# A fused attention and feed-forward kernel: first h of chunk 0 taken ahead, fp32 dummies, a new order at the end of chunk 0, and kv and num rows of 66 columns for 65

## Chip, cores, metric

One core of one Trainium2 chip. The metric is device time in microseconds (us) of one execution. The profile's "span" is about 1.8 us shorter than that time: it leaves out what lies before the first and after the last recorded instruction.

## The reference

```python
# attention with a cosine weight, linear in the sequence: B, H, S, D = 8, 8, 576, 64
theta = pi/2 * arange(S) / S
phi(x) = concat([relu(x)*cos(theta), relu(x)*sin(theta)])     # 2*64 features
kv  = einsum('bhsf,bhsd->bhfd', phi(k), v)
num = einsum('bhsf,bhfd->bhsd', phi(q), kv)
den = einsum('bhsf,bhf->bhs',  phi(q), sum_s phi(k)) + 1e-6
x   = (num/den) as (4608, 512)
# feed-forward: d_model 512, d_ff 2048
h = x @ w_in;  g = h * sigmoid(beta*h);  out = g @ w_out
```

## The kernel before

The 4608 tokens go through the feed-forward part in nine chunks of 512 (chunk 0 to 8), and PE has the attention of the next batch cut in between the chunk's matmuls. A chunk has 32 slots: 16 groups of h (four matmuls of 512 columns each) and 16 of o. The parts that the change and the argument touch:

```python
E = D + 1                       # a row of kv or num: 64 values and the sum for den

def kv_mm(b, jp, bank):         # 72 matmuls a batch, 64x64, 2*E = 130 columns
    ...
def num_mm(n, jp, bank, slot):  # four 64x64 quadrants of PE, cosine half then sine half
    for cs in range(2):
        for jj in range(2):
            for g in range(2):
                nc.tensor.matmul(ps[cols, bank + jj, slot*E : (slot+1)*E],
                                 lhsT=(qt, qs)[cs][rows, jp, n, cols],
                                 rhs=kv[rows, g, jp, cs, :], start=(cs == 0), stop=(cs == 1))

HB = (0, 1, 4, 5)               # PSUM banks of h
def h_bank(c, jt):
    return ((3, 2, 6, 7), (2, 3, 0, 1))[c][jt] if c < 2 and jt < 4 else HB[jt % 4]

def o_part(c, tt, part):        # four of the sixteen matmuls of one o tile;
    ...                         # after the last part ScalarE copies it out (o_sb), then a store

warm_pe(58, 48)                 # PE dummies while the first loads come
...
for gj in GJ: cast_win(0, gj, "pool", jps=slice(0, 1))        # first w_in to bf16, GpSimd
x_turn_pe(0, 0, 8, 2, jps=(0,))                               # x of chunk 0, behind num 1
...
early = { ...
    26: lambda: (takes.append(q_turn_pe(1, 1, 6, hold=True)),
                 [takes[0](*t) for t in turns], cast_wout(3, "addd"),   # last quarter of w_out
                 [takes[1](*t) for t in turns]),
    28: lambda: (num_seven(0, 4), x_mul(x_rden(4, 0, 0, 7, (0,)), 0, 7)),
    29: lambda: (num_seven(1, 6), x_mul(x_rden(6, 0, 0, 7, (1,)), 0, 7)),
    30: lambda: x_turn_pe(1, 0, 7, 4, ("act",), (0,)),        # x of chunk 1
    31: ... }
for slot in range(32):          # chunk 0
    if slot < 4:    h_mm(0, slot, (2, 3)); h_act(0, slot)
    elif slot < 16: h_group(0, slot)
    else:           o_part(0, slot % 4, (slot - 16) // 4)     # w_out arrives by quarters
    ...
    if slot in early: early[slot]()
```

## Time and profile before

| what | before |
|---|---|
| device time | 296.05 us, median of 3 (295.56 to 296.68) |
| span of the profiled run | 294.3 us |
| PE busy | 284.1 us, 97% |
| a chunk in the steady part (chunks 2 to 6) | 30.34 us |
| last quarter of w_out landed, first matmul on it | 45.20 us, 45.99 us |

First the start: PE's timeline. The columns are start (us), length (us, up to the modelled end of the last one), engine, line, operation, destination <- sources, shapes, and the count of instructions run together.

```profile
16.29 0.62 PE L340 MATMUL ps<-ident,xs 128*128 128x128 bf16 x8
...
18.02 0.59 PE L366 MATMUL ps<-xt,win 128*128 128x512 bf16 x2
```

L340 turns x, L366 is h. The first h starts at 18.02. Then the busy time of the engines in the stretch around the end of chunk 0, where the prediction finds its three holes (columns: window; its length, then busy us and instructions of PE, of PE's weight loads, of VectorE, ScalarE and GpSimd; granted clock; DMA share; GB/s):

```profile
45.00:57.00 12.00, 10.74 (x194) 5.51 (x195) 8.31 (x18) 7.26 (x12) 4.33 (x8) 1.00 0.86 317
```

PE is idle for 1.26 us of these 12.

### The profile page before, as it was taken

The page shows a single profiled execution, that of the slowest core. Times are in us where ns is not written, and L with a number is a line of the kernel's source. Part 1 is how long each engine was busy: PE and PEld are TensorE (multiplying, and loading weights), DVE is VectorE, ACT ScalarE, POOL GpSimd, SP SyncE. Part 2 cuts the span into 40 slices and gives each one's busy share as a digit, 9 for nine tenths or more (in the row PEclk, how much of TensorE's full clock was granted, in tenths as well). Part 3 has the DMA queues.
Part 4 walks back from the last instruction along what each step waited for, and adds up shares of the span by engine and source line. Part 5 has one row for each costly group of instructions (what it writes and reads, how often), then busy time and mean ns, then how long its engine had stood idle before and what let it go on. Part 6 is the DMA issues. An engine that isn't in the chain of part 4 may idle for free.

```text
span 294.3 us, 7183 instructions
## 1 busy us (share of the span) xinstructions
PE 284.1 (97%) x3046; PEld 143.2 (49%) x3074; DVE 116.6 (40%) x297; ACT 140.1 (48%) x223; POOL 73.8 (25%) x88
## 2 busy tenths in 40 slices
PE   8799999999999999999999999999999999999995
PEld 7454455455444544454444544554455444444444
DVE  5989968662920294009500860077005000000000
ACT  5768826572248214831384128511761177127611
POOL 1350003252382026402460156014701210000000
PEclk9999999999999999999999999999999999999999
DMA  7999999597898089925992599239201910131033
GB/s 258 373 391 381 389 390 391 192 286 275 159 280 348 2 110 222 374 86 111 210 392 79 102 226 379 82 63 181 64 2 33 159 37 0 38 71 36 0 73 72
DMA packets 50416, 53.82 MB, mean 183 GB/s; under 512 B 30912, under 2 KB 31312, under 8 KB 50384
## 3 DMA queue, kind: packets, MB, share of 16 engines
q1 hardware_dynamic: 47424, 45.88, 51.7%
q0 software_dynamic: 2688, 7.34, 10.1%
q8 instruction: 24, 0.39, 0.5%
q10 hardware_dynamic: 272, 0.14, 0.2%
q14 instruction: 8, 0.07, 0.1%
HBM read 36.71 MB, written 9.44 MB: 157 GB/s over the span
## 4 chain that ended last, share of the span: by engine, by line
PE 84%; DVE 5%; DMA 5%; ACT 2%; issue 2%
PE ps L366 38%; PE ps L391 37%; DMA w_stage<-in_moe_w_out_dram 5%; DVE win L108 4%; PE ps L281 4%; PE ps L260 3%; PE ps L406 1%; PE ps L415 1%; ACT vb L213 1%; DVE qs L218 1%; DVE xs L303 0%; ACT g_t L373 0%; ACT rk L188 0%; PE ps L424 0%; PE ps L230 0%
## 5 line engine op out<-in xcount | busy, mean ns | idle before, releaser
L366 PE MATMUL ps<-xt,win 128*128 128x512 bf16 x576 | 128.1, 379 | 0.7 <-ACT g_t L373 0.5
L391 PE MATMUL ps<-wout,g_t 128*128 128x512 bf16 x535 | 120.4, 379 | 2.5 <-issue 1.4
L373 ACT ACTIVATE g_t<-ps,beta 128x512 bf16<-128x512 f32 x144 | 98.5, 688 | 36.5 <-PE ps L366 36.5
L366 PEld LDWEIGHTS <-win 128*128 128x128 bf16 x576 | 55.3, 98 | 67.5 <-DVE win L108 1.4
L391 PEld LDWEIGHTS <-g_t 128*128 128x128 bf16 x560 | 54.0, 98 | 64.0 <-issue 0.5
L386 POOL DMA_DIRECT2D out_dram<-o_sb x56 | 36.5, 656 | 142.2 <-ACT o_sb L397 142.2
L397 ACT COPY o_sb<-ps 128x512 f32<-128x512 f32 x35 | 20.5, 587 | 98.2 <-PE ps L391 98.2
L218 POOL TENSOR_TENSOR qs<-qt,tanr 128x1152 bf16<-128x1152 bf16 x12 | 29.2, 2456 | 10.3 <-DVE vb L215 8.9
L272 DVE CAST kv<-ps 128x520 bf16<-128x520 f32 x6 | 4.2, 699 | 67.8 <-PE ps L260 67.8
L409 DVE COPY o_sb<-ps 128x256 f32<-128x256 f32 (+1 forms) x2 | 0.7, 358 | 62.6 <-PE ps L406 62.6
L303 DVE TENSOR_TENSOR xs<-ps,rden 128x768 bf16<-128x768 f32 (+5 forms) x26 | 23.1, 890 | 0.8
L292 DVE TENSOR_TENSOR den<-ps,eps 128x12 f32<-128x12 f32 (+4 forms) x26 | 4.2, 161 | 33.5 <-PE ps L281 33.5
L215 DVE TENSOR_SCALAR vb<-raw_v,cos 128x256 bf16<-128x256 f32 x63 | 17.1, 348 | 0.0
L215 DVE TENSOR_SCALAR vb<-raw_v,sin 128x256 bf16<-128x256 f32 x54 | 14.7, 350 | 0.0
L281 PEld LDWEIGHTS <-qt 64*64 64x64 bf16 x576 | 10.6, 106 | 5.0 <-issue 4.3
L281 PE MATMUL ps<-kv,qt 64*64 64x65 bf16 x576 | 11.8, 194 | 0.4 <-ACT kv L270 0.2
L190 DVE TENSOR_SCALAR qb<-raw_q 128x1152 bf16<-128x1152 f32 x16 | 11.4, 753 | 1.3 <-DMA raw_q<-in_q_dram 1.3
L108 DVE CAST win<-w_stage 64x512 bf16<-64x512 f32 (+1 forms) x28 | 11.6, 413 | 0.6
L281 PE MATMUL ps<-kv,qs 64*64 64x65 bf16 x576 | 11.6, 193 | 0.0
L260 PE MATMUL ps<-vb,rk 64*64 64x130 bf16 x576 | 10.0, 218 | 1.6 <-ACT rk L188 1.6
L260 PEld LDWEIGHTS <-rk 64*64 64x64 bf16 x576 | 8.5, 106 | 5.6 <-issue 3.0
L281 PEld LDWEIGHTS <-qs 64*64 64x64 bf16 x576 | 10.4, 105 | 0.0
(56 smaller groups left out, 99.3 us busy)
## 6 DMA issues: line engine op xcount, KB each, us to landing
raw_v<-in_v_dram SPq DMA_DIRECT2D x7, 1152.0 KB, 10.3
raw_k<-in_k_dram SPq DMA_DIRECT2D x7, 1152.0 KB, 12.7
raw_q<-in_q_dram SPq DMA_DIRECT2D x7, 1152.0 KB, 7.5
out_dram<-o_sb POOLq DMA_DIRECT2D x56, 128.0 KB, 4.0
w_stage<-in_moe_w_out_dram SPq DMA_DIRECT2D x4, 1024.0 KB, 9.1
w_stage<-in_moe_w_in_dram SPq DMA_DIRECT2D x3, 1024.0 KB, 13.0
out_dram<-o_sb SPq DMA_DIRECT2D x14, 128.0 KB, 2.3
raw_q<-in_q_dram SPq DMA_DIRECT2D x2, 576.0 KB, 4.4
```

The source lines that it names most:

```text
L108: nc.vector.tensor_copy(o, a)
L190: nc.vector.tensor_scalar(dst, src, scalar1=0.0, scalar2=None, op0=ALU.max)
L215: nc.vector.tensor_scalar(o, a, scalar1=t[:, n : n + 1], scalar2=None, op0=ALU.mult)
L218: eng.tensor_tensor(dst.rearrange("q n (g p) -> q n g p", g=2), src.rearrange("q n (g p) -> q n g p", g=2), tanr[:, n0:n1].unsqueeze(2).to ...
L260: nc.tensor.matmul(t[jj * HP : (jj + 1) * HP, g], lhsT=rk[hs, n, 2 * jp + jj, :], rhs=vb[hs, n, 2 * jp + jj].rearrange("q s e -> q (s e)") ...
L281: nc.tensor.matmul(ps[cols, bank + jj, slot * E : (slot + 1) * E], lhsT=(qt, qs)[cs][rows, jp, n, cols], rhs=kv[rows, g, jp, cs, :], start ...
L303: nc.vector.tensor_tensor(o.rearrange("q j n s d -> q j (n s) d"), nv[:, :, a:z, :, 0:D].rearrange("q j n s d -> q j (n s) d"), rden[:, :, ...
L366: nc.tensor.matmul(ps[:, h_bank(c, jt)], lhsT=win[jt // 4][:, mi, (jt % 4) * P : (jt % 4 + 1) * P], rhs=xt[:, :, jp, g * HP : (g + 1) * HP ...
L373: nc.scalar.activation(g_t, ps[:, h_bank(c, jt)], AF.Silu, scale=beta[:, jt : jt + 1])
L386: eng.dma_start(out=out_v[bb, n][:, m0:m1], in_=o_sb[hf * HP : (hf + 1) * HP, m0:m1])
L391: nc.tensor.matmul(o_ps, lhsT=gs[c, jt][:, tt * P : (tt + 1) * P], rhs=wout[jt // 4][:, jt % 4, :], start=(jt == 0), stop=(jt == JT - 1))
L397: nc.scalar.copy(o_sb, o_ps)
```

## The change

Its intent: start h of chunk 0 earlier (fp32 dummies fill PE before that), close the holes where chunk 0 passes into chunk 1, and make the rows of kv and num an even number of columns so that all of them start on an even address.

```diff
-    E = D + 1
+    E = D + 2
+    nc.vector.memset(vb.rearrange("q n j s e -> q (n j s) e")[:, :, D + 1], 0.0)
@@ banks of h
-        return ((3, 2, 6, 7), (2, 3, 0, 1))[c][jt] if c < 2 and jt < 4 else HB[jt % 4]
+        if c < 2 and jt < 4:
+            return ((3, 2, 0, 1), (6, 7, 2, 3))[c][jt]
+        return ((6, 7, 4, 5) if c == 0 else (4, 5, 0, 1))[jt % 4]
@@ start
-    warm_pe(7)
+    warm_long(4)                          # four fp32 matmuls of 256 columns
...
+    x_turn_pe(0, 0, 4, 4, jps=(0,))       # x of chunk 0 ahead of num 1
+    x_turn_pe(0, 4, 8, 5, jps=(0,))
     for n in range(7):
         num_mm(n, 1, 0, n)
     num_mm(7, 1, 6, 0)
-    for gj in GJ:
-        cast_win(0, gj, "pool", jps=slice(0, 1))
...
-    x_turn_pe(0, 0, 8, 2, jps=(0,))
+    for gj, eng in zip(GJ, ("pool", "dve", "pool", "dve")):
+        cast_win(0, gj, eng, jps=slice(0, 1))
+    for gj, eng in zip(GJ, ("dve", "pool", "pool", "pool")):
+        cast_win(0, gj, eng, jps=slice(1, 2))
...
@@ end of chunk 0
-        [takes[0](*t) for t in turns], cast_wout(3, "addd"),
+        [takes[0](*t) for t in turns], cast_wout(3, "adda"),
-    30: lambda: x_turn_pe(1, 0, 7, 4, ("act",), (0,)),
...
+        elif slot < 28:
+            o_part(0, slot % 4, (slot - 16) // 4)
         else:
-            o_part(0, slot % 4, (slot - 16) // 4)
+            for tt in (2 * (slot % 2), 2 * (slot % 2) + 1):
+                o_mm(0, tt, range(12, 14) if slot < 30 else range(14, 16),
+                     (lambda: x_turn_pe(1, 0, 7, 4, ("act",), (0,))) if tt == 0 else None)
```

(Cut: h in two blocks of columns, the split of v's scaling, slots 4 and 9 for 3 and 7, num_rest in bank 0, three fewer dummies, and the place of a few VectorE casts.)

## The prediction

> **What bounds the kernel now.** I read the page first, then the chain of waits, then the timelines of the stretches that the change touches.
>
> ```profile
> span 294.3 us, 7183 instructions
> PE 284.1 (97%) x3046; PEld 143.2 (49%) x3074; DVE 116.6 (40%) x297; ACT 140.1 (48%) x223; POOL 73.8 (25%) x88
> PE   8799999999999999999999999999999999999995
> DMA  7999999597898089925992599239201910131033
> ```
>
> PE is at work from end to end; no other engine is near it. From chunk 2 on the chain is PE alone, one chunk every 30.34 us (124 to 154 us, say), with no wait but the switches between the 128-wide and the 64-wide matmuls. So a gain can only be work taken from PE, or a PE hole closed in the first 57 us. The second thing to see is the DMA row: sevens and nines in its first seven slices, the first 50 us. There the kernel also loads 15 MB. The chain of waits, in order of time, says what that does:
>
> ```profile
> 31.44 13.76 DMA w_stage<-in_moe_w_out_dram
> 45.22 0.73 ACT wout L115
> 45.99 1.02 PE ps L391 x4
> ...
> 50.16 0.46 issue
> 50.62 0.92 ACT xt L345
> 51.59 1.02 PE ps L366 x4
> ...
> 55.27 1.27 ACT g_t L373 x2
> 56.59 7.93 PE ps L366 x36
> ```
>
> Three PE holes stand here. By the starts of the matmuls: one of 0.385 us before 45.99 (start-to-start 601 ns where 216 is the pace), where PE wants the last quarter of w_out, landed at 45.20 and scaled on ScalarE until 45.94; one of 0.39 us before 51.59 (606 ns), PE waiting for ScalarE's copy of x of chunk 1, which had stood behind a copy of o_sb; and one of 0.655 us before 56.59 (871 ns), PE waiting for a silu to release bank 0. Ahead of 45.99 the load is no bubble: its issue at 31.44 queues behind others. The landings before it come at 33.06, 36.08, 38.78, 41.80 and 45.20, each about 3 us for about 1 MB, and the bandwidth stays at 380 to 400 GB/s. The first 45 us are therefore a race of two streams, and the DMA stream wins it by 0.385 us.
>
> For the rows of 65 I looked at the 64-wide matmuls of one steady chunk; four quadrants run side by side, so a line of four is one step:
>
> ```profile
> 101.42 0.20 PE L281 MATMUL ps<-kv,qt 64*64 64x65 bf16 x4
> 101.45 0.20 PE L281 MATMUL ps<-kv,qs 64*64 64x65 bf16 x4
> 101.49 0.20 PE L281 MATMUL ps<-kv,qt 64*64 64x65 bf16 x4
> 101.52 0.20 PE L281 MATMUL ps<-kv,qs 64*64 64x65 bf16 x4
> 101.55 0.20 PE L281 MATMUL ps<-kv,qt 64*64 64x65 bf16 x4
> ...
> 101.68 0.20 PE L281 MATMUL ps<-kv,qt 64*64 64x65 bf16 x4
> ```
>
> Eight steps from 101.42 to 101.68, some 32 ns each. In nanoseconds the steps repeat with a period of four: 29, 35, 33, 32. Of these the 29 is the cosine half (a kv row at an even column) into an even slot of PSUM; the three others have an odd start in kv, in PSUM, or in both.
>
> **What the Trainium skill says.** (1) TensorE: Matmul & The Clock Gate, Back-to-back issue gap: a warm matmul of N columns takes N/2.4 + 2.5 ns. The trace agrees: 216 ns at 512, 56 at 128, and the kv steps of 130 columns 56.7. For 65 it gives 29.6, which only the aligned step shows. (2) Advanced Engine Details and Errata, PSUM Cachelines and SBUF Cachelines: PSUM lines are 8 bytes, two fp32 values, and SBUF lines 16 bytes. It doesn't say what an odd start costs; the 29 against 32 to 35 above fits it, with two causes not told apart. (3) Advanced Engine Details and Errata, VectorE Performance Modes: the two-port mode wants SBUF on both sides and even outer dimensions. So I do not expect rows of 66 to speed up the scaling of v: its 256 columns at 348 ns are 215 ns fixed and 133 at two a cycle, the same fixed part as 482 ns for 512 columns of wout gives, so it is fast already. (4) DMA: Bandwidth & Descriptors, Issuing engines are not separate DMA queues: all loads share the same 16 engines and interleave, from which I take it that an earlier issue into a full queue brings nothing. The row of nines agrees.
>
> **The change part by part.**
>
> *Rows of 66.* A num step becomes (66+6)/2.4 = 30.0 ns, always aligned, against a mean of 32.3 in the first 20 steps of a chunk and 33.4 in the last 16 (mean 32.8): 2.8 x 36 = 0.10 us less per batch. A kv step goes from 56.7 to 57.5 (two more columns): 0.8 x 18 = 0.015 more. Net 0.085 us per batch; batch 0 lies ahead of the DMA wait, so seven count: -0.6 us. The added memset (72 columns; a 64-column one took 0.11 us) falls into VectorE's 0.38 us idle before 4.36. The copies of kv, 528 columns for 520, are some 8 ns longer.
>
> *Start of chunk 0.* Before: x of the first half goes through PE at 16.29, ScalarE copies it until 18.0, h starts at 18.02, and the sixteen matmuls of the first four h groups end at 21.9. After: x is transposed in two parts ahead of num 1 (VectorE's product, 1.08 us from 14.35, is split as well), ScalarE copies from about 15.6 to 16.8 in two copies of 0.59, and the four casts of w_in that it needs (0.61 each on GpSimd, from 14.87) are shared with VectorE (0.42). So h may start at about 16.9. VectorE pays: three casts ahead of den of num 1 move that from 16.36 to about 16.8, so x of the second half is there at 20.0, against 19.5 before; the split of h into blocks lets half of the rest begin at 19.3. I get the sixteen done at about 21.0: 0.9 us earlier. GpSimd's two added slices of v (1.47 us becomes 1.96) end at 10.9, where k, landed 10.30, holds ScalarE's relu until about 11.1 anyway. The fp32 dummies fill a stretch in which PE waits. Then the sum: of these 0.9 us, nothing arrives. PE then stands before w_out's last quarter 1.3 us instead of 0.385, since the load still lands near 45.2 (15 MB at the same rate, same order of issue) and the first cast still ends at 45.94. I set this part at 0.
>
> *End of chunk 0, start of chunk 1.* From 45.99 on PE has the same matmuls in another order. The first two of each o group go first, and the transposes of x stand after the first group's last two, at about 49.5, with ScalarE's copy ahead of all o_sb copies. That copy is done at about 51.0 while PE is busy until 51.2: the hole of 0.39 closes. Chunk 1's first groups use banks 6, 7, 2, 3 and the fifth bank 4, idle since that copy: the hole of 0.655 closes. Given back: ScalarE now has two casts of w_out (0.63 apart) ahead of the second q copies; VectorE loses one of 0.4, but waits for ScalarE at the last piece, so qs ends at 48.0 rather than 47.83 and the product for x about 0.2 later, of which some 0.1 reaches PE. Net -0.9 us.
>
> Sum: -0.6 - 0.9 = -1.5 us, 296.05 to 294.5.
>
> **The rivals.** (a) The early start does come through, because w_out lands sooner. For it: that landing took 3.4 us where 1 MB usually takes 2.7, with an instruction fetch of 16 KB at 42.9 on one DMA engine, so the landing can move by 0.7. Against: PE's program has as many instructions, so the fetch comes again. It would give 293.6. (b) The holes after 46 us only shift: VectorE's product for x becomes the wait at 49.5, or the fifth h waits for something else. ScalarE is at 4 us in 5 there, but not full. It would give 295.3. (c) The slow num steps come from the weight loads of 64 columns, not from odd starts, so that 66 is no better and costs 0.12 us of kv and 0.1 of num in all. Against: the 29 ns step has the same weight loads. It would give 295.3. (d) PE gets behind: a VectorE cast waiting for the second part of w_in (landed 16.18) holds x of num 1. It has over 1 us of slack at the DMA wait, so it would cost nothing.
>
> **Range and chances.** The middle is 294.5. Rivals a, b and c span 293.6 to 295.3, and single runs of the kernel before span 1.1 us, so 293.5 to 295.6 should hold it 8 times in 10. Faster by over 2% would be under 290.1, over four times the gain that I find anywhere: 0.02. Slower by over 2% needs a new wait of 6 us: 0.02. Within 2%: 0.96.
>
> **What would show it.** Num steps at 30 ns without the period of four; steady chunks at 30.25 us instead of 30.34; the first h at about 16.9 and the fifth h group at about 21; a PE hole before the last quarter of w_out that has grown to over 1 us, with that matmul again at about 46.0; no holes of 0.4 us at 51 and 0.65 at 56. I am wrong if that matmul starts well before 45.5, if num steps stay at 32 to 33, or if chunk 1's fifth h group still waits for ScalarE.

## The result, and the profile after

The changed kernel took 295.96 us, median of four runs (295.83 to 296.0); the kernel before 296.0 (295.56 to 296.68). A ratio here is the mean time of one kernel's fast runs over the mean of the other's in the same rounds, so not quite the ratio of the medians: 0.9996, 95% interval 0.9976 to 1.0015. That is the same within 2%, as predicted, but the time lies outside the predicted range of 293.5 to 295.6. Of the 1.5 us, next to nothing arrived.

Lines of the page after, for those that the prediction shows of before:

```profile
span 294.1 us, 7240 instructions
PE 285.8 (97%) x3080; PEld 144.4 (49%) x3080; DVE 116.8 (40%) x297; ACT 139.7 (47%) x223; POOL 74.3 (25%) x85
```

The chain of waits after, in order of time (start, length, what):

```profile
30.95 14.29 DMA w_stage<-in_moe_w_out_dram
45.26 0.73 ACT wout L115
46.04 1.02 PE ps L392 x4
...
51.42 0.86 PE ps L367 x4
...
54.37 9.17 PE ps L367 x42
...
101.70 1.62 PE ps L392 x7
103.93 9.87 PE ps L392 x45
...
132.83 11.33 PE ps L392 x52
```

Up to 54.37 this is the prediction: w_out again lands at 45.24 and sets PE's start at 46.04; then no copy of x at 50.6 and no silu at 55.3 stands in the chain any more. (The 54.37 here is a modelled time; by its start it is 54.30. The same matmul started at 54.63 before, and after six matmuls PE waited until 56.59 for the silu.) The stretch's busy time says the same:

```profile
45.00:57.00 12.00, 11.59 (x200) 5.85 (x199) 8.14 (x17) 8.00 (x14) 4.58 (x8) 1.00 0.89 299
```

PE now idles 0.41 us in it instead of 1.26; what is left is the wait for w_out. (The two windows don't hold quite the same work; by the same matmul, the first of kv in chunk 2, the kernel after is 1.07 us ahead: 93.83 against 94.90.)

The unexpected thing is one line further down. The last 52 matmuls of o of a chunk run in one piece in chunks 3 to 6 ("x52"), but in chunk 2 they are broken at the eighth, 101.70 to 103.93. PE's timeline there:

```profile
101.64 1.69 PE L392 MATMUL ps<-wout,g_t 128*128 128x512 bf16 x7
103.93 2.32 PE L392 MATMUL ps<-wout,g_t 128*128 128x512 bf16 x10 [0.61 <-issue]
```

The seventh starts at 102.94, the eighth at 103.93: 986 ns where 216 is the pace, so 0.77 us are lost inside one accumulation, with weights, operands and bank long there. "issue" means that the profile finds nothing that PE waited for. But the DMA view of 101.2 to 102.6 us holds one packet, and it isn't data:

```profile
q8 instruction: 1, 0.02, 5.6%
```

5.6% of 16 engines over 1.4 us is 1.25 us of one engine: an instruction fetch of 16 KB, from 101.28 to 102.52 in the trace. The kernel before has one too, at 102.33 to 103.55, and no hole behind it. After this hole the lead is 0.30 us (kv of chunk 3 at 124.95 against 125.25).

One half of the num matmuls, by groups, first before, then after (columns: busy us, mean ns of one from its own start to its end, so not the pace):

```profile
L281 PE MATMUL ps<-kv,qt 64*64 64x65 bf16 x576 | 11.8, 194 | 0.4 <-ACT kv L270 0.2
L282 PE MATMUL ps<-kv,qt 64*64 64x66 bf16 x576 | 11.7, 195 | 0.2 <-ACT kv L271 0.2
```

The busy time is as good as unchanged. Counted by starts, the 144 num matmuls of a steady chunk take 1.237 us before and 1.237 us after, and the steps still repeat 29, 35, 33, 32 ns. The 72 of kv take 0.999 us before and 1.012 us after.

The start after, on PE:

```profile
16.82 1.03 PE L367 MATMUL ps<-xt,win 128*128 128x512 bf16 x4
18.65 0.40 PE L341 MATMUL ps<-ident,xs 128*128 128x128 bf16 x4 [0.81 <-DVE xs L304]
```

The first h is at 16.82, as predicted (16.9), but then PE loses 0.97 us waiting for VectorE's x (the profile counts 0.81 idle, as ends are modelled). By the starts of the matmuls, the first four h groups are done at 21.94, not at the predicted 21.0, and even 0.2 us later than before (21.74). The first o of chunk 0 is at 32.77 instead of 32.99, and PE stands before the last quarter of w_out at 45.46 instead of 45.605: inside, 0.15 us arrived where 0.9 was predicted, and the hole before w_out is 0.58 us instead of the predicted 1.3.

The whole account, in us, between the two profiled runs:

| term | predicted | measured |
|---|---|---|
| rows of 66: num | -0.7 | 0.00 |
| rows of 66: kv | +0.1 | +0.09 (seven times 0.013) |
| start of chunk 0 | 0 | 0 |
| end of chunk 0 | -0.9 | -1.05 |
| last quarter of w_out, first matmul on it | 0 | +0.05 |
| hole in chunk 2 | not in the sum | +0.77 |
| a like stall in chunk 1, only before | not in the sum | -0.11 |
| sum | -1.5 | -0.25 |
| span | | -0.22 (294.27 to 294.05) |

The stall in chunk 1 is in num: 1.351 us before and 1.238 after; before, PE stops there for 0.11 us, 1.4 us after a fetch landed at 70.65. 0.03 us of the difference of the spans are not accounted for.

### The profile page after: what moved, and what is told of

Its sections match the earlier page's. It is cut to its first block, busy times and chain, and to the rows that moved or that the text cites. A ratio compares the mean times of both kernels' runs of the same rounds, so it can differ in the third digit from the quotient of the medians.

```text
span 294.1 us, 7240 instructions
## 1 busy us (share of the span) xinstructions
PE 285.8 (97%) x3080; PEld 144.4 (49%) x3080; DVE 116.8 (40%) x297; ACT 139.7 (47%) x223; POOL 74.3 (25%) x85
## 4 chain that ended last, share of the span: by engine, by line
PE 83%; DMA 8%; DVE 5%; issue 1%; SPq 1%; ACT 1%
PE ps L392 38%; PE ps L367 38%; DMA w_stage<-in_moe_w_out_dram 5%; DVE win L108 4%; PE ps L282 3%; DMA raw_v<-in_v_dram 3%; PE ps L261 2%; PE ps L412 1%; DVE xs L304 1%; SPq L78 1%; ACT vb L214 0%; DVE rden L297 0%; PE ps L341 0%; ACT wout L115 0%; DVE den L293 0%
## 5 line engine op out<-in xcount | busy, mean ns | idle before, releaser
L367 PE MATMUL ps<-xt,win 128*128 128x512 bf16 (+1 forms) x584 | 127.8, 376 | 0.1
L392 PE MATMUL ps<-wout,g_t 128*128 128x512 bf16 x560 | 124.7, 379 | 1.0 <-issue 0.6
L367 PEld LDWEIGHTS <-win 128*128 128x128 bf16 x584 | 56.4, 98 | 65.1 <-issue 0.4
L387 POOL DMA_DIRECT2D out_dram<-o_sb x56 | 38.0, 683 | 145.7 <-ACT o_sb L400 145.7
L273 DVE CAST kv<-ps 128x528 bf16<-128x528 f32 x6 | 4.2, 707 | 67.9 <-PE ps L261 67.9
L219 POOL TENSOR_TENSOR qs<-qt,tanr 128x1152 bf16<-128x1152 bf16 x12 | 28.5, 2398 | 6.4 <-DVE vb L216 6.3
L108 DVE CAST win<-w_stage 64x512 bf16<-64x512 f32 x27 | 12.0, 443 | 0.6
L191 DVE TENSOR_SCALAR qb<-raw_q 128x1152 bf16<-128x1152 f32 x16 | 11.4, 752 | 1.3 <-DMA raw_q<-in_q_dram 1.3
L261 PE MATMUL ps<-vb,rk 64*64 64x132 bf16 x576 | 10.3, 219 | 1.7 <-DVE rk L191 0.8
L282 PE MATMUL ps<-kv,qt 64*64 64x66 bf16 x576 | 11.7, 195 | 0.2 <-ACT kv L271 0.2
L282 PE MATMUL ps<-kv,qs 64*64 64x66 bf16 x576 | 11.5, 193 | 0.0
```

The lines of the kernel that those rows point to most:

```text
L108: nc.vector.tensor_copy(o, a)
L191: nc.vector.tensor_scalar(dst, src, scalar1=0.0, scalar2=None, op0=ALU.max)
L219: eng.tensor_tensor(dst.rearrange("q n (g p) -> q n g p", g=2), src.rearrange("q n (g p) -> q n g p", g=2), tanr[:, n0:n1].unsqueeze(2).to ...
L261: nc.tensor.matmul(t[jj * HP : (jj + 1) * HP, g], lhsT=rk[hs, n, 2 * jp + jj, :], rhs=vb[hs, n, 2 * jp + jj].rearrange("q s e -> q (s e)") ...
L282: nc.tensor.matmul(ps[cols, bank + jj, slot * E : (slot + 1) * E], lhsT=(qt, qs)[cs][rows, jp, n, cols], rhs=kv[rows, g, jp, cs, :], start ...
L367: nc.tensor.matmul(ps[:, h_bank(c, jt), blocks.start * 64 : blocks.stop * 64], lhsT=win[jt // 4][:, mi, (jt % 4) * P : (jt % 4 + 1) * P], ...
```

## The experiments

Two questions: is the hole in chunk 2 the fetch, and why do rows of 66 do nothing? For the hole, theory 1: a line of 256 PE instructions comes late, so the hole stands at a fixed count of instructions and moves when PE has more or fewer of them ahead of it. The rival: the hole belongs to what the change does with data (the wider rows, the new banks), and then goes away with that and not with the count. For the rows, the prediction's step (an odd start costs, so an even one gains) stands against its own rival (c): the weight loads of 64 columns set the pace. A third question, later: is the early start really worth nothing, or only because something else is in the way?

"Faster", "same" and "slower" below are ratios to the kernel before in the same rounds; none reaches 2%, so all are "same" in the class of the prediction. Runs a were on one chip, b and d1 on a second, c on a third: compare runs of different letters by the ratio. What every run gave:

| run | median us (runs) | ratio to before, 95% interval | loss at the hole in chunk 2 |
|---|---|---|---|
| a1_after_again | 295.71 (5) | 0.9979, 0.9966 to 0.9992 | 0.45 us, eighth o matmul |
| a2_rows65 | 295.54 (5) | 0.9981, 0.9969 to 0.9993 | 0.48 us, eighth |
| a3_before_rows66 | 295.75 (5) | 0.9994, 0.9982 to 1.0005 | none |
| a4_shift64 | 298.03 (6) | 1.007, 1.0048 to 1.0092 | none |
| b1_end_only | 294.87 (6) | 0.9954, 0.994 to 0.9968 | none (0.18 in chunk 5) |
| b2_dummies51 | 297.44 (6) | 1.0047, 1.0029 to 1.0064 | none |
| b3_dummies63 | 295.26 (4) | 0.9971, 0.9953 to 0.999 | none |
| b4_sine40 (wrong result) | 296.2 (1) | | 1.08 us, eighth |
| c1_start_only63 | 295.91 (5) | 0.9996, 0.9981 to 1.0011 | 0.27 us, third |
| c2_fill | 294.99 (6) | 0.996, 0.9943 to 0.9978 | none |
| c3_casts_pool | 295.63 (1) | | 0.32 us, fourth |
| d1_start_fill | 295.19 (6) | 0.9973, 0.9958 to 0.9988 | 0.32 us, third |

### a1: the changed kernel again

No edit; five rounds, for the size of the difference and to see whether the hole comes again.

> The changed kernel once more, for a second profile and a narrow interval. In its first profile PE was 1.05 us ahead of the kernel before from 57 us on, and lost 0.77 us of it in one hole at 103 us, between two matmuls of one group. Theory 1 (a hole of the instruction supply, tied to the place in the program): the hole is there again, at 103 us, 0.6 to 0.9 us long; time 295.9. Theory 2 (a chance event): no hole there, or one elsewhere; then 295.2. Theory 3 (the profile of before was a slow sample and there is no gain at 57 us): the fifth group of h in chunk 1 starts less than 0.5 us ahead of the kernel before in the same job.

295.71 us (294.99 to 295.96): faster by 0.2%, and this interval leaves 1 out. The hole is there again, ahead of the same eighth matmul: the seventh starts at 103.14, the eighth 668 ns later, 0.45 us lost (0.6 to 0.9 was expected). So it is no accident of one execution, and its size varies: the fetch was from 101.45 to 102.41.

### a2 and a3: the rows alone

```diff
 # a2: the changed kernel
-    E = D + 2
+    E = D + 1
-    nc.vector.memset(vb.rearrange("q n j s e -> q (n j s) e")[:, :, D + 1], 0.0)
 # a3: the kernel before
-    E = D + 1
+    E = D + 2
+    nc.vector.memset(vb.rearrange("q n j s e -> q (n j s) e")[:, :, D + 1], 0.0)
```

> The changed kernel with rows of 65 again and without the memset; all else as changed. If rows of 66 cost nothing but two more columns in kv, kv takes 0.999 us for 72 matmuls rather than 1.012 and the num phase 1.237 us as with 66; time 0.1 us below the changed kernel (295.8). If odd starts cost what the prediction said, the num phase is 0.1 us longer than with 66: the two profiles already speak against it. The PE hole at 103 us: with theory 1 at the same place (the PE program is unchanged, row for row); with theory 2 it need not be.

> The kernel before with rows of 66 alone. Only kv grows, 13 ns per batch: 296.1, so same within noise. The prediction's step of -0.6 us would give 295.4; a num phase at 1.14 us rather than 1.237 would be its sign, and I no longer expect that.

Both give 1.237 us for the num phase of a steady chunk, with 65 columns as with 66; kv takes 0.999 us with 65 and 1.012 with 66. The hole is in a2 (rows of 65, ahead of the eighth matmul) and not in a3 (rows of 66), so it isn't the rows. a3 has the two holes of the old end of chunk 0 again, 0.389 and 0.653 us. Its 295.75 against 296.08 leave 1 inside the interval: rows of 66 alone are worth nothing that can be told from zero.

### a4 and b2: more and fewer instructions ahead

```diff
 # a4: the changed kernel
     warm_long(4)
+    warm_pe(32, 32)          # 64 PE instructions more
 # b2: the changed kernel
-    warm_pe(58, 48)
+    warm_pe(51, 55)          # 14 fewer, about the same time
```

> The changed kernel with 32 more dummies of 32 columns in a stretch of the start in which PE waits for k (idle from 10.0 to 10.84 us). They cost nothing there (32 x 25 ns = 0.8 us, before a wait of which PE has over 0.5 us to spare at the wait for w_out), but move all later PE instructions 64 places on. Theory 1: the hole at 103 us moves or goes; if it goes, 295.2. Theory 2: no telling. If PE is just late by the dummies: no change of the time, since the wait for w_out takes it.

> The changed kernel with 51 dummies of 55 columns in place of 58 of 48 at the very start: as many columns, 14 PE instructions fewer, so that those of chunk 2 stand where they stand in the kernel before. Theory 1 (the hole at 103 us depends on where the num phase of chunk 2 lies in the blocks of 256 instructions in which they are fetched): no hole, 0.45 to 0.77 us less than the changed kernel, 295.2. If the hole had to do with anything else that the change did (banks, order, rows of 66), it stays, and 295.9.

In both the hole in chunk 2 is gone, as theory 1 has it, but both missed on the time: 298.03 and 297.44 us, slower by 0.7% and 0.5%. A hole stands in the start instead, behind another fetch, and costs more there. The PE timeline of b2 shows it inside the 36 matmuls of one kv:

```profile
14.09 0.62 PE L261 MATMUL ps<-vb,rk 64*64 64x132 bf16 x20 [0.51 <-ACT rk L189]
17.10 0.66 PE L261 MATMUL ps<-vb,rk 64*64 64x132 bf16 x16 [2.39 <-issue]
...
20.08 1.91 PE L367 MATMUL ps<-xt,win 128*128 128x512 bf16 x4
```

The fetch there ran from 14.55 to 15.68. In a4 the hole is 2.3 us, from 16.6 on:

```profile
19.05 1.50 PE L367 MATMUL ps<-xt,win 128*128 128x512 bf16 x4 [2.10 <-DVE xs L304]
```

with the fetch from 16.48 to 17.57. (VectorE, the releaser named, can't be what held it: this is the first h, which in the changed kernel starts at 16.82 with the same casts done.) And there is a second cost: the clock falls to half and PE runs at half pace until about 23 us, 427 ns for a matmul of 512 columns (in b2 the four of 20.08). The granted clock of b2 shows it, in the page's row of 40 slices; the third is 14.8 to 22.2 us:

```profile
PEclk9969999999999999999999999999999999999999
```

### b3: ten instructions more

```diff
-    warm_pe(58, 48)
+    warm_pe(63, 44)
```

> The changed kernel with 63 dummies of 44 columns, 10 PE instructions more. Theory 1 says more here: the hole stays at the same instruction of the program's count, so it moves from ahead of the eighth o matmul after num of chunk 2 to ahead of the third, some 1.1 us earlier in chunk 2, and is again 0.4 to 0.8 us long, because the fetch starts as much earlier. Time as the changed kernel, 295.7 to 296.0. A hole still ahead of the eighth speaks against it.

295.26 us. The expected hole ahead of the third matmul was not in this profile: its fetch was at 99.22, before num began, instead of 101.28. c1, c3 and d1 have the same 63 dummies, and there it is, ahead of the third or fourth matmul, so five (in c3 four) matmuls of two instructions each earlier than the eighth: where ten more instructions ahead put it (in c3 eight more, as PE has two semaphore waits fewer ahead).

With all runs that have the hole, in us:

| run | fetch landed | PE goes on | between | PE instructions ahead |
|---|---|---|---|---|
| after | 102.52 | 103.93 | 1.41 | 2753 |
| a1 | 102.41 | 103.81 | 1.40 | 2753 |
| a2 | 101.75 | 103.12 | 1.37 | 2753 |
| b4 | 102.92 | 104.35 | 1.43 | 2753 |
| c1 | 101.43 | 102.88 | 1.45 | 2753 |
| c3 | 101.49 | 102.86 | 1.37 | 2753 |
| d1 | 100.71 | 102.04 | 1.33 | 2753 |
| b2, in the start | 15.68 | 17.10 | 1.42 | 450 |
| a4, in the start | 17.57 | 19.05 | 1.48 | 707 |
| b1, in chunk 5 | 192.25 | 193.59 | 1.34 | 4802 |

The last column counts PE's records in the trace (matmuls, weight loads, semaphore waits) that start before the matmul that goes on. It is the same in all seven runs with the hole in chunk 2, whatever their order, banks and rows are, and the four numbers differ by multiples of 256, within two (2753 - 450 is 9 x 256 - 1). That is theory 1 in the traces themselves: PE stands where one line of 256 gives way to the next. The stalls in num of chunk 1 (0.01 to 0.08 us in a2, b3 and c1) stand behind 1985 instructions, 3 x 256 fewer than 2753.

PE goes on 1.33 to 1.48 us after the fetch has landed, wherever it lies. In b3 that would be about 101.5, and its third matmul was due at about 101.67, so no hole. In the kernel before, the fetch landed at 103.55, ready at about 104.95 by the same rule; PE has 14 instructions fewer ahead, so the place is the fifteenth matmul, due at about 105.7: no hole either. The changed kernel's 14 more instructions bring the place forward by seven matmuls, 1.5 us, and that is more than there was in hand. Why the place after num is the tight one is argued, not shown: num's 144 matmuls and 144 loads pass in 1.237 us, so that 256 instructions last about 1.1 us there (an estimate from this), no longer than a fetch.

### b4: num with 40 columns in the sine half (wrong result)

If odd starts or the number of columns set the pace of num, steps of 40 columns must be much shorter. The result is wrong (relative error 0.38).

```diff
+                    e0 = 26 * cs
-                        ps[cols, bank + jj, slot * E : (slot + 1) * E],
+                        ps[cols, bank + jj, slot * E + e0 : (slot + 1) * E],
-                        rhs=kv[rows, g, jp, cs, :],
+                        rhs=kv[rows, g, jp, cs, e0:E],
```

> Wrong on purpose: the changed kernel with the sine half of num adding only 40 of its 66 columns. If a num step is set by the columns that it streams, sine steps fall from 33 ns to (40+6)/2.4 = 19 ns, the num phase from 1.237 us to about 1.0. If it is set by the weight loads, the sine steps stay at 32 to 35 ns and the phase at 1.237 us; then neither rows of 66 nor starts at even columns could have made it faster.

The num phase took 1.234 us instead of 1.237. PE's timeline:

```profile
101.28 0.22 PE L283 MATMUL ps<-kv,qt 64*64 64x66 bf16 x4
101.31 0.21 PE L283 MATMUL ps<-kv,qs 64*64 64x40 bf16 x4
101.34 0.22 PE L283 MATMUL ps<-kv,qt 64*64 64x66 bf16 x4
```

Steps of 40 and of 66 columns alternate, and each takes 31 to 34 ns; by columns the 40 would take 19. So neither the columns nor the even start sets the pace. (The period of four is gone here, 31 or 32 ns in most of the first 20 steps, while the sum stays: what makes that pattern is open.) What stays is the stream of weight loads, one of 64 columns for each matmul; that they are the bound is the one explanation left of those considered, not something that a run took away. A rival to it was not tested: the rate at which PE takes instructions, eight a step, so about 4.1 ns each.

### b1: the end of chunk 0 alone

The kernel before, with its start and rows of 65, and only the new banks of chunk 1's h, the new order of o, the transposes of x between, num_rest in bank 0 and the last cast on ScalarE.

```diff
-    26: ... cast_wout(3, "addd"), ...
+    26: ... cast_wout(3, "adda"), ...
-    30: lambda: x_turn_pe(1, 0, 7, 4, ("act",), (0,)),
+        else:                             # slots 28 to 31
+            for tt in (2 * (slot % 2), 2 * (slot % 2) + 1):
+                o_mm(0, tt, range(12, 14) if slot < 30 else range(14, 16), ...)
```

> The kernel before with only the end of chunk 0 changed (order of the last o matmuls, x transposed ahead of the o_sb copies, other banks for chunk 1, casts of w_out). Its PE program has as many instructions ahead of chunk 2 as the kernel before, so no hole at 103 us is expected (theory 1). If this part is the whole gain, the two holes of 0.39 and 0.65 us at 51 and 56 us go and the time is 1.0 us below the kernel before: 295.0. If the new start is needed for it, less than 0.5 us.

294.87 us (294.34 to 295.29), faster by 0.46% (0.3 to 0.6): the lowest ratio of all versions (the interval of c2 overlaps it), better than both kernels. No hole at 51, at 56 or in chunk 2, in PE's timeline:

```profile
50.08 1.46 PE L391 MATMUL ps<-wout,g_t 128*128 128x512 bf16 x6
51.37 1.03 PE L366 MATMUL ps<-xt,win 128*128 128x512 bf16 x4
...
101.72 3.63 PE L391 MATMUL ps<-wout,g_t 128*128 128x512 bf16 x16
```

PE has as many instructions ahead of chunk 2 as the kernel before (1214 weight loads ahead of its num in both; 1220 in the changed kernel, and these six pairs of load and matmul with two more waits are its 14), so the fetch is in time. This is the predicted -0.9 by itself: -1.17 by the medians (296.04 to 294.87).

### c1: the start and the rows, without the end

The changed kernel with the old end of chunk 0 and 63 dummies.

```diff
-            return ((3, 2, 0, 1), (6, 7, 2, 3))[c][jt]
-        return ((6, 7, 4, 5) if c == 0 else (4, 5, 0, 1))[jt % 4]
+            return ((3, 2, 0, 1), (2, 3, 0, 1))[c][jt]
+        return ((6, 7, 4, 5) if c == 0 else (0, 1, 4, 5))[jt % 4]
-    warm_pe(58, 48)
+    warm_pe(63, 44)
...  # and the hunk "end of chunk 0" of the change taken back
```

> The changed kernel with the end of chunk 0 as before (order, banks, casts), and with 63 dummies of 44 columns, whose count showed no hole in chunk 2: so the new start, the fp32 dummies and rows of 66 alone. The prediction set the start at 0 because PE waits for the last quarter of w_out anyway. If that holds: 296.0, same as the kernel before within 0.2%, with both holes of 0.39 and 0.65 us at 51 and 56 us back. If the start brings something of its own: 295.5 or less.

295.91 us against 296.25, ratio 0.9996: the start is worth nothing that can be told from zero. The chain shows the two old waits, ScalarE's copy of x and the silu:

```profile
50.17 0.92 ACT xt L346
...
51.14 1.02 PE ps L367 x4
...
54.82 1.27 ACT g_t L374 x2
```

(lost: 0.391 and 0.655 us, as before the change). In this profile w_out landed at 44.61, and PE didn't wait for it; what an earlier landing gave, the hole of 0.27 us in chunk 2 and kv's wider rows took in part.

### c3: all eight casts of the first w_in on GpSimd

Why did the early start arrive only with 0.15 us? In the changed kernel VectorE's timeline has its three casts at 15.59, beside GpSimd's:

```profile
15.59 1.93 DVE L108 CAST win<-w_stage 64x512 bf16<-64x512 f32 x3
```

They took 0.42, 0.72 and 0.72 us, where 0.42 each was predicted, so den came at 17.44 instead of 16.8. GpSimd's own went from 0.61 to between 0.69 and 0.77.

```diff
-    for gj, eng in zip(GJ, ("pool", "dve", "pool", "dve")):
+    for gj, eng in zip(GJ, ("pool", "pool", "pool", "pool")):
         cast_win(0, gj, eng, jps=slice(0, 1))
-    for gj, eng in zip(GJ, ("dve", "pool", "pool", "pool")):
+    for gj, eng in zip(GJ, ("pool", "pool", "pool", "pool")):
         cast_win(0, gj, eng, jps=slice(1, 2))
```

(with 63 dummies)

> The changed kernel, 63 dummies, with all eight casts of the first part of w_in on GpSimd. In the changed kernel VectorE's three casts beside GpSimd's took 0.42, 0.72 and 0.72 us and GpSimd's 0.69 to 0.77 where they take 0.42 and 0.61 alone. If the two hinder each other, GpSimd's casts are back at 0.61 us here, and VectorE's den of num 1 starts at about 16.4 to 16.8 us rather than at 17.4; h then starts at about 17.7 for want of GpSimd's fourth cast. If the casts are slow for another reason (the load of w_in landing at the same time), GpSimd's casts stay at 0.7 us.

VectorE's timeline in c3, the den of num 1:

```profile
16.69 0.17 DVE L293 TENSOR_TENSOR den<-ps,eps 128x14 f32<-128x14 f32 x1 [1.09 <-PE ps L282]
```

GpSimd's casts went back to 0.60 to 0.61 us and den to 16.69. But the first h at 16.85 then waits 0.67 us for GpSimd, so little is won inside; VectorE's later casts of w_in were again slow (0.85, 0.74) as long as GpSimd worked beside them, and 0.42 when it had stopped. The two engines hinder each other here; dividing the casts between them doesn't give the sum of their speeds. The time, 295.63 in one run, can't tell anything.

### c2 and d1: filling the wait for w_out

If PE stands before w_out, give it other work. The num of the first half of batch 1 goes ahead of the last quarter of o. c2 has this on top of b1 (old start), d1 on top of the new start with rows of 65 and 63 dummies.

```diff
-            return ((...), (6, 7, 2, 3))[c][jt]
+            return ((...), (4, 2, 3, 6))[c][jt]
     26: lambda: (..., [takes[0](*t) for t in turns], cast_wout(3, "adda"),
-                 [takes[1](*t) for t in turns]),
-    28: lambda: (num_seven(0, 4), x_mul(x_rden(4, 0, 0, 7, (0,)), 0, 7)),
-    29: lambda: (num_seven(1, 6), x_mul(x_rden(6, 0, 0, 7, (1,)), 0, 7)),
+    27: lambda: (num_seven(0, 4), x_mul(x_rden(4, 0, 0, 7, (0,)), 0, 7),
+                 [takes[1](*t) for t in turns]),
+    30: lambda: (num_seven(1, 6), x_mul(x_rden(6, 0, 0, 7, (1,)), 0, 7)),
```

> A version that should beat both: the kernel before with the changed end (which gave 294.87), and num of batch 1's first half (0.68 us of PE work that needs no w_out) moved ahead of the wait for w_out, VectorE's product for x with it; chunk 1's first four groups in banks 4, 2, 3, 6 so that none waits for num's second half. PE has some 0.3 to 0.6 us to fill there, so 294.3 to 294.6. If the product for x or the second q copies become the wait instead, 294.9 as without it.

> The changed kernel with rows of 65, 63 dummies in place of 58, and the num of the first half of batch 1 moved from behind the last quarter of w_out to ahead of it (about 0.9 us of PE work), so that PE has something to do while it waits there. In runs with the new start PE arrives at 45.46 and waits 0.15 to 0.7 us, depending on when the load lands; in the run with the old start and the same filling there was nothing to fill, and it gained nothing over the end alone (294.99 against 294.87). If the early start of 0.15 us plus the wait can be turned into work, this gives 294.4: no PE hole over 0.1 us at 45 to 46, and the fifth h group of chunk 1 0.3 to 0.5 us earlier against the landing than in the changed kernel. If VectorE and ScalarE, which have to copy q and cast w_out in the same 2 us, set the end of chunk 0 instead, PE waits again at 47 to 50 and it gives 294.9 to 295.3, no better than the end alone. The hole of the fetch in chunk 2: 0 to 0.3 us with 63 dummies.

c2 missed: 294.99, no better than b1's 294.87 (ratios 0.996 and 0.9954). With the old start PE reaches w_out when its cast is as good as done, so there is no wait to fill. d1 missed its 294.4 too: 295.19, inside the range of its rival theory but not for the rival's reason. The mechanism did work in its profile, as PE's timeline shows (the num in front of 46.28 begins at 45.64):

```profile
46.28 2.32 PE L391 MATMUL ps<-wout,g_t 128*128 128x512 bf16 x10
...
53.97 3.19 PE L366 MATMUL ps<-xt,win 128*128 128x512 bf16 x14
...
101.28 0.60 PE L391 MATMUL ps<-wout,g_t 128*128 128x512 bf16 x2
102.04 3.18 PE L391 MATMUL ps<-wout,g_t 128*128 128x512 bf16 x14 [0.16 <-issue]
```

PE is busy for 12.00 us of the 12 from 45 to 57, h is back at 53.97 where b1 has 54.41, and then the fetch takes 0.32 us of the 0.44 in chunk 2. The medians still differ by 0.3 us the other way. A part of it is the clock: two of d1's six executions and three of c2's six have a mean granted clock of 0.993 or 0.994, none of b1's is under 0.998; the others alone have medians of 294.98 (d1), 294.75 (c2) and 294.87 (b1). What the rest is I can't say; the intervals of d1, c2 and b1 overlap, and the landing of w_out moves all of them by up to 1 us from run to run (between 44.5 and 45.5). No version with the new start was faster than the end alone.

## Why the prediction was wrong

The class (the same within 2%) was right, the size wrong. Step by step:

**Rows of 66: this step failed.** It put "the three others have an odd start" behind the steps of 32 to 35 ns and counted on 30.0 ns with even starts. The runs show 1.237 us for a num phase with either row, and still with 40 columns in half of the steps. The prediction had named this sign itself ("if num steps stay at 32 to 33"). Its rival (c) fits: 66 is no better, with the cost in kv that it named (0.09 measured for 0.12) and without its 0.1 in num; that the weight loads are the reason stays unproven (b4). The error was in the reading of the skill: "TensorE: Matmul & The Clock Gate", section Back-to-back issue gap, says that the pace of a stream of loads and matmuls is set by both, and that the formula N/2.4 + 2.5 is for an isolated matmul and counts too little at small N. The prediction took the formula because it fitted 56 ns at 128 columns, where the loads hide, and carried it to 65 columns, where the runs don't bear it out. The one step of 29 ns in four looked like proof; it repeats in a pattern that a row of 66 doesn't change, so it isn't the alignment.

**Start of chunk 0: worth 0, right; its inner 0.9 us, wrong.** c1 shows no gain with the start alone. Of the 0.9 us inside only 0.15 came: the term that was mis-sized is VectorE's casts beside GpSimd's, 0.42, 0.72 and 0.72 for three times 0.42, so that den came 0.6 us late. c3 took that away and won little, as h then waited for GpSimd. The skill has it: "Advanced Engine Details and Errata", VectorE Performance Modes, Mode Summary, says that VectorE's second port to SBUF is shared with GpSimd and that the two block each other. The prediction had quoted that section for another purpose. So the 0 is right partly by luck: the wait for w_out, which was to swallow 0.9 us, had 0.15 to swallow, and no run shows that it would have swallowed the rest.

**End of chunk 0: right.** Predicted -0.9, measured -1.05: both holes closed, nothing given back. b1 has it alone.

**What was left out: the fetch.** The prediction even saw "an instruction fetch of 16 KB at 42.9", but only as a load on a DMA engine, and said of PE's program that it "has as many instructions". It has 14 more ahead of chunk 2, and these moved the place where PE runs out of instructions seven matmuls forward, in front of the end of a fetch. +0.77 us in the first run, +0.45 in its repeat. That the place follows the count is shown by b3's family, by a4 and b2, and by the count itself. Not shown is what decides when a fetch starts (99.2 to 102.3 in chunk 2), and what PE does in the 1.33 to 1.48 us after it has landed.

Together: with -1.05 from the end alone the time would have been near 294.9, inside the range. The prediction added 0.6 that isn't there, and missed 0.5 to 0.8 that is.

## What to carry to other kernels

Before you change the shape of a narrow matmul, ask whether its columns set the pace at all; a test with far fewer columns tells it in one run. On a kernel whose PE has no slack, count PE's instructions as well as its time: a few dummies more or fewer can move a fetch stall from a place where it costs nothing to one where it costs half a microsecond, or two and a half, so look at the instruction queue of the DMA view whenever PE stops on "issue" in the middle of a group. And when a change has several parts, run each alone: here one part was worth 1.2 us and the rest took most of it back.

## What the Trainium skill lacked or had wrong

- No page says what a late fetch costs PE. "Runtime: NRT & Kernel Launch", Instruction fetch mechanics, calls the cost of crossing a block of 256 instructions mostly hidden and names a stall only after a taken branch; none of PE's records here is a branch. Here fetches of 16 KB took 0.88 to 1.78 us, and in ten places PE went on 1.33 to 1.48 us after the landing; the holes were 0.27 to 1.08 us in chunk 2, and 2.3 and 2.4 us in the start.
- "TensorE: Matmul & The Clock Gate", Back-to-back issue gap, warns that loads count at small N, but has no figure for a stream of 64x64 quadrants: four side by side took 31 to 34 ns a step with 40 columns, as with 66. Its own sustained figures (about 81 ns at 128 columns, 131 at 512) aren't met here: transposes of 128 columns with a load each ran at 57 ns (seven from 49.57 to 49.97), matmuls of 512 at 216.
- "Advanced Engine Details and Errata", PSUM Cachelines and SBUF Cachelines, doesn't say what an odd start costs: no run here shows any cost of it; 65 and 66 columns gave 1.237 us for 144 matmuls.
- "TensorE: Matmul & The Clock Gate", The HAM clock gate, puts the fall to half clock after an idle window of about 3.4 us. In b2 the granted clock was 0.50 from 16.44 to 23.27 us, although PE had been busy for 1.17 of the 3.41 us before that; in c2 it was 0.50 from 11.4 to 14.8, after 1.43 of 3.40 us busy.
